# A gated mix of a long convolution and a dense ReLU block: three eras instead of two, the last one's first layer by Strassen products

## The chip, the cores and the metric

The kernel runs on one core of a Trainium2 chip. The metric is the device time of one execution in microseconds (us), the median of several runs. The engines are named as in the profile: PE is TensorE's matmuls, PEld its weight loads, DVE is VectorE, ACT ScalarE, POOL GpSimd, SP the engine that issues the DMAs.

## The reference

Tokens S = 2048, channels D = 512, hidden width 1792, all in float32. Cut to what matters:

```
k_shift = sum over t in 0..3 of k_pad[:, t:t+S, :] * shift_k[:, 3-t]     # causal taps
kv = k_shift * v
y  = causal convolution over S of kv with ssm_k, per channel (by FFT of length 2S)
a  = q * (y + kv * ssm_D)
b  = relu(q @ w1) @ w2                       # x of both branches is q
g  = sigmoid((q * gate_w).sum(-1))
out = g * a + (1 - g) * b
```

## The kernel before, in words

**Dense branch.** The 2048 tokens are four chunks of 512, the hidden width 14 blocks of 128. A float32 matrix is split into a high and a low part with short mantissas (`split`, L295: the high part by a cast on ScalarE, L299; the low part by a subtraction on VectorE or, as its `alt`, on POOL, L302), and each product is three matmuls: high by high, high by low, low by high. `mlp1` (L369) computes one hidden block for one chunk: 4 k parts by 3 matmuls of 128x128 by 128x512, 12 in all, L376 to L378. `mlp1_out` applies ReLU: ScalarE writes the high part `hh` (L389), VectorE the low part `hl` (L392). `mlp2` (L398) computes 128 tokens by 512 outputs of one chunk, adding up over the blocks of the era, 3 matmuls a block, L406 to L408. An era is a set of blocks: there are two of 7 (`ERAS`, L292), the second runs over the chunks in reverse (`CHUNKS`, L293), so the chunk at the turn needs no new load of x. Results of the first era are copied to `y` by ScalarE (L421); those of chunk 0 go out to DRAM (`yd`, L426) and come back before the end (`again`, L790). In the second era VectorE adds to `y` (L429), except for the last chunk, whose results are used from PSUM.

**Convolution branch.** It runs beside the dense one as a transform in steps. `conv_x` (L491) forms taps and product on VectorE; `stage1` (L451) transforms h and x of 8 groups by small tiled matmuls (L459) and stores to the DRAM buffer `sa`. `conv_mid` (L558) runs for 8 groups of frequencies: forward matmuls `f_h` and `f_x` (L575, 64 together), complex products on VectorE (L609, L617), their sums on POOL (L623), and, two groups later, the inverse `iv` (L652, 32 matmuls), whose results `bv` leave PSUM half by ScalarE (L662), half by VectorE (L664) to the DRAM buffer `sb`. A closing call takes the last two inverses in one go. `conv_end` (L687) loads from `sb`, runs the last small matmuls `cy` (L727) in two runs of 8 groups, and forms gate and output on VectorE (L709, L737, L740, L677).

**Order.** All operations are entered in a list with a cost, a rank, dependencies and buffers, and `Plan.order` (L97) runs a list schedule over them by its cost constants: at each instant the engine takes the ready operation of lowest rank. The program is then written in that order, so each engine's queue is static. Dense matmuls have ranks (1, count); conv matmuls rank (0, ...), so they go first once ready. A pair of stage-one operations waits, up to `LONG` by the planner's clock, for a partner and for the end of a `mlp2` run (`twin`, L113), because tiled matmuls are costly to switch to. Buffers are rings, named by tag, with the counts in `room`; a ring with `fifo` is filled in the order in which its users were entered. There are eight PSUM banks (`cv`). Conv tiles lie in a pool that `phase` (L435) swaps: phase 1 for stage one (input ring `in`, 7 tiles), phase 2, after the last store to `sa`, for the middle (`r` 4 and `yr` 2 tiles), phase 3, after the last store to `sb`, for the end (`br`, 4 tiles of 8 KB per partition).

## Time and profile before

| what | value |
|---|---|
| median of 3 runs | 385.86 us (385.71 to 385.87) |
| span of the profiled execution, first to last instruction | 384.2 us |
| mean granted clock of TensorE in it | 0.999 |
| DMA in it | 92.51 MB, mean 241 GB/s |
| busy: ACT | 128.8 us |
| busy: POOL | 91.5 us |

The profiled execution's own time is known only as its span; the median of the timed runs is 1.66 us above that. In the profile "L376" is line 376 of the kernel, "x160" a count, and an arrow names what is written and what is read. In the rows by line, busy time and mean duration of one instruction (ns) are followed by the idle time ahead of them and by what ended it. In the rows by stage each engine has its busy time and, in brackets, its instructions; the last three numbers are the granted clock, the busy share of the DMA engines and GB/s. Rows of the timeline give start, duration, engine, line and operation.

### The profile page before, as it was taken

Reading aid. Unit: us, or ns where it says so; the run is one execution under the profiler, and the core shown is the slowest. Engines: PE = TensorE matmul, PEld = TensorE weight load, DVE = VectorE, ACT = ScalarE, POOL = GpSimd, SP = SyncE. Lnnn points to the kernel's source line nnn. Section 1 sums busy time; section 2 is a strip of 40 time slices with the busy share of each in tenths; the row PEclk is TensorE's granted clock in tenths of the full one; section 3 lists DMA queues with packets and bytes.
Section 4 is the critical chain, followed back from the end, with each engine's and each line's share of the span. In section 5 each row is a group of like instructions: output and inputs, shape, how many; then the busy total and the mean of one; then the engine's idle time right before and its main releaser. Section 6 shows DMA issues by size and latency. Waiting matters only on the chain.

```text
span 384.2 us, 6567 instructions
## 1 busy us (share of the span) xinstructions
PE 379.8 (99%) x2505; PEld 273.8 (71%) x2505; DVE 266.7 (69%) x356; ACT 128.8 (34%) x242; POOL 91.5 (24%) x77
## 2 busy tenths in 40 slices
PE   9999999999999999999999999999999999999996
PEld 5888788668877788788655765565587788688684
DVE  4698999797989028114799687897872347687691
ACT  5643524573147525533224022313400333012100
POOL 0000000000000000000199968866995001000000
PEclk9999999999999999999999999999999999999999
DMA  7997893898648763589867876686460798399331
GB/s 274 368 317 255 298 351 113 293 333 323 208 121 330 295 234 109 185 296 275 285 203 238 307 265 227 241 308 232 139 204 3 241 342 320 120 325 357 117 124 56
DMA packets 43474, 92.51 MB, mean 241 GB/s; under 512 B 4625, under 2 KB 7201, under 8 KB 43442
## 3 DMA queue, kind: packets, MB, share of 16 engines
q1 hardware_dynamic: 43090, 91.77, 68.8%
q8 instruction: 20, 0.33, 0.4%
q10 hardware_dynamic: 288, 0.26, 0.2%
q14 instruction: 12, 0.10, 0.1%
q0 software_dynamic: 64, 0.05, 0.0%
HBM read 61.66 MB, written 30.41 MB: 240 GB/s over the span
## 4 chain that ended last, share of the span: by engine, by line
PE 99%; DVE 0%; DVEq 0%; issue 0%
PE m L406 14%; PE m L407 13%; PE m L408 13%; PE m L376 13%; PE m L377 12%; PE m L378 12%; PE iv L652 4%; PE f_h L575 4%; PE f_x L575 4%; PE m L362 3%; PE s1x L459 2%; PE s1h L459 2%; PE cy L727 2%; PE warm L753 1%; DVE o L677 0%; DVEq L887 0%
## 5 line engine op out<-in xcount | busy, mean ns | idle before, releaser
L623 POOL TENSOR_TENSOR p<-p,ha 128x512 f32<-128x512 f32 x32 | 41.1, 1308 | 202.2 <-DVE ha L617 201.6
L406 PE MATMUL m<-w1h_h,hh 128*128 128x512 f32 x224 | 88.7, 396 | 0.0
L407 PE MATMUL m<-w1l_l,hh 128*128 128x512 f32 x224 | 87.3, 390 | 0.0
L408 PE MATMUL m<-w1h_h,hl 128*128 128x512 f32 x224 | 87.2, 389 | 0.0
L389 ACT ACTIVATE hh<-m 128x512 fp32r<-128x512 f32 x56 | 33.1, 598 | 126.4 <-PE m L378 122.1
L392 DVE SCALAR_TENSOR_TENSOR hl<-m,hh 128x512 fp32r<-128x512 f32 x56 | 38.3, 688 | 44.5 <-ACT hh L389 44.3
L376 PE MATMUL m<-xh_h,w0h_h 128*128 128x512 f32 x160 | 63.0, 394 | 0.0
L377 PE MATMUL m<-xl_l,w0h_h 128*128 128x512 f32 x160 | 62.3, 390 | 0.0
L378 PE MATMUL m<-xh_h,w0l_l 128*128 128x512 f32 x160 | 62.3, 389 | 0.0
L406 PEld LDWEIGHTS m<-w1h_h,hh 128*128 128x128 f32 x224 | 42.0, 188 | 19.1 <-ACT ev L464 6.5
L408 PEld LDWEIGHTS m<-w1h_h,hl 128*128 128x128 f32 x224 | 42.0, 188 | 9.0
L407 PEld LDWEIGHTS m<-w1l_l,hh 128*128 128x128 f32 x224 | 42.1, 188 | 8.3
L376 PEld LDWEIGHTS m<-xh_h,w0h_h 128*128 128x128 f32 x160 | 30.0, 188 | 11.1 <-issue 4.2
L378 PEld LDWEIGHTS m<-xh_h,w0l_l 128*128 128x128 f32 x160 | 30.0, 188 | 6.4
L377 PEld LDWEIGHTS m<-xl_l,w0h_h 128*128 128x128 f32 x160 | 30.0, 188 | 6.0
L518 DVE TENSOR_TENSOR acc<-acc,tmp 128x1024 f32<-128x1024 f32 x24 | 29.3, 1222 | 0.6
L302 DVE TENSOR_TENSOR w1l_l<-raw,w1h_h 128x512 fp32r<-128x512 f32 x14 | 9.4, 686 | 17.7 <-ACT w1h_h L299 17.7
L662 ACT COPY bv<-iv 128x512 f32<-128x512 f32 x16 | 8.7, 589 | 37.1 <-PE iv L652 31.9
L515 DVE TENSOR_TENSOR tmp<-in,sht_sht 128x512 f32<-128x512 f32 x32 | 20.8, 685 | 0.1
L623 POOL TENSOR_TENSOR p<-p,qa 128x512 f32<-128x512 f32 x16 | 20.7, 1317 | 0.0
L617 DVE TENSOR_TENSOR ha<-f_x,ha 128x1024 f32<-128x1024 f32 x16 | 19.5, 1221 | 1.3 <-DVE qb L617 0.5
L623 POOL TENSOR_TENSOR p<-p,qb 128x512 f32<-128x512 f32 x16 | 20.3, 1290 | 0.0
(72 smaller groups left out, 468.1 us busy)
## 6 DMA issues: line engine op xcount, KB each, us to landing
sa<-ev SPq DMA_DIRECT2D x64, 256.0 KB, 3.0
sb<-bv SPq DMA_DIRECT2D x32, 256.0 KB, 3.4
br<-sb SPq DMA_DIRECT2D x16, 512.0 KB, 6.8
raw<-xp SPq DMA_DIRECT2D x28, 256.0 KB, 4.2
raw<-w SPq DMA_DIRECT2D x24, 256.0 KB, 3.8
r_x<-sa SPq DMA_DIRECT2D x12, 512.0 KB, 5.1
in<-kn SPq DMA_DIRECT2D x10, 512.0 KB, 5.0
r_h<-sa SPq DMA_DIRECT2D x10, 512.0 KB, 6.3
```

The lines of the kernel that those rows point to most:

```text
L376: mm(ps, part("h", f, k), T["x", "h", xe, c, k], start=k == 0, stop=False)
L377: mm(ps, part("h", f, k), T["x", "l", xe, c, k], start=False, stop=False)
L378: mm(ps, part("l", f, k), T["x", "h", xe, c, k], start=False, stop=k == 3)
L389: nc.scalar.activation(tile_of(("hh", era, c, f), "hh", dt=F32R, p=mp, bufs=HB), T["m1", era, c, f], AF.Relu)
L392: nc.vector.scalar_tensor_tensor(tile_of(("hl", era, c, f), "hl", dt=F32R, p=mp, bufs=HB), T["m1", era, c, f], 0.0, T["hh", era, c, f].bit ...
L406: mm(ps, T["hh", era, c, f][:, z], T["w", "h", 1, f], start=f == fs[0], stop=False)
L407: mm(ps, T["hh", era, c, f][:, z], T["w", "l", 1, f], start=False, stop=False)
L408: mm(ps, T["hl", era, c, f][:, z], T["w", "h", 1, f], start=False, stop=f == fs[-1])
L515: nc.vector.tensor_tensor(o[:, z], T["k", c + (j == 0) + part][:, u], T["sht",][:, j * D:(j + 1) * D], op=OP.mult)
L518: nc.vector.tensor_tensor(T["acc", c], T["acc", c], T[dst], op=OP.add)
L575: mm(ps[b][32 * j:32 * j + 32, :], T[k("cf")][at, 64 * j + 32 * o:64 * j + 32 * o + 32], T[k("r", t, j // 2)][at, (j % 2) * D:(j % 2 + 1) ...
L623: nc.gpsimd.tensor_tensor(planes("p", dst, n), planes("p", dst, n), planes(src, u, n), op=OP.add if sign > 0 else OP.subtract)
```

## The change

There are three eras, of 5, 5 and 4 blocks; the second goes backwards over the chunks and the third forwards again. The second layer accumulates once per era. `y` stays in SBUF; the trip of chunk 0 through DRAM goes. In the third era the first layer isn't computed by `mlp1` but by `combine`, for each pair of chunks (c, d). There the weights of two blocks are seen as a 2 x 2 matrix A (blocks by halves of k) and x as a 2 x 2 matrix B (halves of k by chunks), and Winograd's form of Strassen's algorithm gives the four results from seven products of 6 matmuls each, for two u (pairs of blocks) in turn. Combinations t1 to t4 of x are formed on VectorE or POOL, s1 to s4 of the weights in `load_combined`, and each is split anew. The sums of products are kept by VectorE in SBUF (u2, u3) or finish a result (c21, c22, c12); p1 is copied by ScalarE. The x of the second pair lies in the phase-3 pool (ring `xs`), the first pair's in the ring `r`.

All conv loads use one ring `r` of 8 tiles of 4 KB outside the phase pools; a `br` load takes two of them. The loads of h and x in the middle wait for the stores of h or of x alone. The two closing inverses are separate calls, all `bv` leave PSUM by ScalarE, two of the sums of the last group run on VectorE, `conv_end` has four runs of 4 groups. Results of chunks 2 and 3 are used from PSUM in the last era. Buffers: `w0` 7 (WA), `w2` 5, `hh` 5, `t` 2, `q` 5. In the planner a waiting stage-one operation wakes when its time in `LONG` is over; the third entry of `LONG` goes from 12 to 0.

```diff
+            if op["pair"]:
+                event(now + LONG[op["pair"] - 1] + 0.01, "wake", op)
...
-    ERAS = [range(0, NF // 2), range(NF // 2, NF)]
-    CHUNKS = [list(range(NCHUNK)), list(range(NCHUNK))[::-1]]
+    ERAS = [range(0, 5), range(5, 10), range(10, NF)]
+    CHUNKS = [[0, 1, 2, 3], [3, 2, 1, 0], [0, 1, 2, 3]]
+    TURN = [None, 3, 0]
...
+    def combine(p, c, d, cgate):
+        pairs = [tuple(ERAS[2][2 * u:2 * u + 2]) for u in range(2)]
...
+        for nm, src, k0 in (("b22", d, 2), ("b12", d, 0), ("b11", c, 0), ("b21", c, 2)):
...
+            raws[nm] = add("SP", ISSUE, (-47, rank[1])[p], go, [cgate if p else xgate[0]], [tag], dma=2 * ROW, fifo=[tag])
...
+            made[dst] = add("DVE", dve_time(2 * D), rank, go, deps, port=True, alt=("POOL", 2.39))
...
+        minus("t3", "b22", "b12", [raws["b22"], raws["b12"]], "b22")
+        minus("t1", "b12", "b11", [made["t3"], raws["b11"]], "b12")
+        minus("t2", "t3", "b11", [made["t1"], *own("b11")], "b11", 1)
+        minus("t4", "b21", "t2", [made["t2"], raws["b21"], *own("b21")], "b21")
...
+        for nm, ld in (("t2", "t4"), ("t3", "t2"), ("t4", "t4"), ("t1", "t2"), ("b22", None)):
+            if not ld:
+                made[ld] = add("SP", ISSUE, rank[-1], again, [cgate, made["t2"]], ["xs"], dma=2 * ROW, fifo=["xs"])
+            for i in range(2):
+                cut(nm, i, made[ld], [tag if ld else "xs"] if i else [])
...
+                    ps = bank(key) if first and not i else T[key]
+                    mm(ps, w_at("h", wn, u, i), x_at("h", xn, i), start=first and not i, stop=False, skip_group_check=True)
+                    mm(ps, w_at("h", wn, u, i), x_at("l", xn, i), start=False, stop=False, skip_group_check=True)
+                    mm(ps, w_at("l", wn, u, i), x_at("h", xn, i), start=False, stop=last and i == 1, skip_group_check=True)
+
+                prev = add("PE", 3 * MM, (1, at[0] - back, u, i), go, [wpart[wn, u], xl[xn, i], prev, *([] if i else deps)],
+                           ["cv"] if first and not i else (), ["x"] if u else (), ends=bool(i))
...
+        x = [product(n("X", u), u, "a11", "b11", [], True, False, 0 if p else BACK) for u in us]
+        p1 = [add("ACT", act_time(D, True), (0, -1000 + at[0]), lambda u=u: nc.scalar.copy(tile_of(n("p1", u), "raw", p=mp), T[n("X", u)]), [x[u]], ["raw"], fifo=["raw"]) for u in us]
...
+        x = [product(n("X", u), u, "a12", "b21", [p1[u]], False, True, 0 if p else BACK) for u in us]
...
+        z = [product(n("Z", u), u, "s2", "t2", [], True, False) for u in us]
+        u2 = [summed(n("u2", u), "raw", n("Z", u), n("p1", u), [z[u], p1[u]]) for u in us]
...
+        z = [product(n("Z", u), u, "s3", "t3", [u2[u]], False, False) for u in us]
+        u3 = [summed(n("u3", u), "sv", n("Z", u), n("p1", u), [z[u], cgate]) for u in us]
...
+        z = [product(n("Z", u), u, "a22", "t4", [u3[u]], False, True) for u in us]
+        c21 = [summed(n("p1", u), None, n("Z", u), n("p1", u), [z[u]], ["cv"]) for u in us]
...
+        for s in range(4):
+            mlp2(2, c, s, [pairs[u][e] for e in range(2) for u in us])
...
+        y = [product(n("Y", u), u, "s1", "t1", [], True, False, 1.5) for u in us]
+        c22 = [summed(n("u3", u), None, n("Y", u), n("u3", u), [y[u]]) for u in us]
...
+        y = [product(n("Y", u), u, "s4", "b22", [c22[u]], False, True) for u in us]
+        c12 = [summed(n("u2", u), None, n("Y", u), n("u2", u), [y[u]], ["cv"]) for u in us]
...
+        for s in range(4):
+            mlp2(2, d, s, [pairs[u][e] for e in (1, 0) for u in us])
...
+    def load_combined(rank):
...
+            s1 = combo("s1", 0, (1, 0), (1, 1), 1, [lg], ["raw"])
+            s3 = combo("s3", 0, (0, 0), (1, 0), -1, [lf, lg, own], ["raw"])
+            s2 = combo("s2", 1, (0,), (0, 0), -1, [s1, lf])
+            s4 = combo("s4", 1, (0, 1), (1,), -1, [s2, s3], (), ["raw"])
...
-            nc.sync.dma_start(rows(tile_of(key, "in", R * D)), src)
+            nc.sync.dma_start(rows(tile_of(key, "r", R * D, p=mp)), src)
...
-            return add("SP", ISSUE, rank + 0.1 * u + (0 if t == "h" else 1), ld, [gate], [tag], dma=2 * ROW, fifo=[tag])
+            return add("SP", ISSUE, rank + 0.1 * u + (0 if t == "h" else 1), ld, stores[t], ["r"], dma=2 * ROW, fifo=["r"])
...
-            if j % 2:
+            if True:
...
-    for g in range(NJ // 4 + 1):
+    for g in range(NJ // 4 + BEHIND):
...
-    for m in range(2):
-        conv_end(order_n[8 * m:8 * m + 8], p3)
+    for m in range(4):
+        conv_end(order_n[4 * m:4 * m + 4], p3)
...
+DIRECT = 2, 3
+BACK = 2.5
+XR = 540.0, 704.5
+WA = 7
-LONG = 50.0, 50.0, 12.0, 0.0
+LONG = 50.0, 50.0, 0.0, 0.0
```

## The prediction

> **What bounds the kernel now.** I read the head of the page first, then the busy time by stage, then TensorE's own timeline, and only after that the groups of the other engines. The page:

> ```profile
> span 384.2 us, 6567 instructions
> PE 379.8 (99%) x2505; PEld 273.8 (71%) x2505; DVE 266.7 (69%) x356; ACT 128.8 (34%) x242; POOL 91.5 (24%) x77
> PE   9999999999999999999999999999999999999996
> PE 99%; DVE 0%; DVEq 0%; issue 0%
> ```

> The chain that ended last is TensorE and nothing else. By stage (0 to 100 us: first stage of the long convolution beside the dense layers; 100 to 183; 183 to 299: its middle; then its end), columns are length, PE, PEld, DVE, ACT and POOL busy:

> ```profile
> 0.00:100.00 100.00, 99.22 (x520) 75.61 (x521) 83.47 (x103) 46.54 (x84) 0.88 (x5) 1.00 0.84 295
> 100.00:183.00 83.00, 83.00 (x457) 64.20 (x456) 41.21 (x54) 38.94 (x72) 0.00 (x0) 1.00 0.66 223
> 183.00:299.00 116.00, 116.00 (x1080) 71.25 (x1078) 90.14 (x93) 28.34 (x51) 89.30 (x71) 1.00 0.64 218
> 299.00:384.20 85.20, 81.57 (x460) 62.78 (x452) 51.92 (x107) 15.02 (x36) 1.29 (x1) 1.00 0.63 226
> ```

> TensorE is full in every stage; VectorE (DVE) is at 83% in the first and 78% in the third. A busy PE could still hide waits shorter than a matmul's modelled end (0.39 us against a spacing of 0.23), so I read starts, not durations:

> ```profile
> 183.08 0.39 PE L378 MATMUL m<-xh_h,w0l_l 128*128 128x512 f32 x1
> 183.40 1.95 PE L575 MATMUL f_h<-r_h,cf 64*32 64x512 f32 x32
> 185.14 1.92 PE L575 MATMUL f_x<-r_x,cf 64*32 64x512 f32 x32
> 187.00 0.50 PE L376 MATMUL m<-xh_h,w0h_h 128*128 128x512 f32 x1
> 187.34 0.40 PE L377 MATMUL m<-xl_l,w0h_h 128*128 128x512 f32 x1
> ...
> 190.34 0.39 PE L378 MATMUL m<-xh_h,w0l_l 128*128 128x512 f32 x1
> ...
> 193.06 0.39 PE L378 MATMUL m<-xh_h,w0l_l 128*128 128x512 f32 x1
> ...
> 380.18 0.39 PE L408 MATMUL m<-w1h_h,hl 128*128 128x512 f32 x1
> 380.61 0.88 DVE L677 SCALAR_TENSOR_TENSOR o<-m,gs,t 128x256 f32<-128x256 f32 x2 [4.01 <-PE m L408]
> ```

> From 190.34 to 193.06 are twelve matmuls: 2.72/12 = 0.2267 us each, the price of a dense matmul. One visit to the convolution's tiled matmuls costs, beyond the matmuls: 183.08 to 183.40 is 0.09 over a step; the second group of 32 takes 1.86 to the next start where the first took 1.74, so 0.12; 187.00 to 187.34 is 0.11 over a step. Together **0.32 us per visit**. After the last matmul starts, 4.0 us remain, which the change leaves. So time is the number of dense matmuls, plus the tiled ones, plus visits, plus whatever waits appear; now there are practically none. The span is 384.2, the median of the timed runs 385.86: 1.66 us lie around the span, and I keep them.

> **The change part by part.**

> *Strassen products (removed: matmuls).* Four blocks over four chunks take 4 x 4 x 12 = 192 matmuls in the first layer. The new form has 7 products of 6 matmuls (two k parts, three high/low terms), for two u and two chunk pairs: 7 x 6 x 2 x 2 = 168. The second layer keeps its count, merely cut into three accumulations per output instead of two. So 24 x 0.2267 = **-5.44 us**, all of it on the bound.

> *More visits (added).* By the kernel's loops there are now 8 in stage one, 8 in the middle, one closing inverse that does two groups, 2 at the end. The closing inverse becomes two visits and the end four (four runs of four instead of two of eight): +3 x 0.32 = **+0.96 us**. Stage one goes in twos (h and x, 32 matmuls a visit); the planner's new "wake" can let one go alone once it has waited 50 us by its clock. Bounds: 0 to 8 more visits, 0 to 2.56 us; I take 0, because rests between second-layer runs become more frequent (a chunk of 5 blocks is 5 x 24 x 0.2267 = 27 us, one of 7 is 38), so pairing gets easier.

> *VectorE and its helpers.* The rows for the sizes that occur:

> ```profile
> L392 DVE SCALAR_TENSOR_TENSOR hl<-m,hh 128x512 fp32r<-128x512 f32 x56 | 38.3, 688 | 44.5 <-ACT hh L389 44.3
> L512 DVE TENSOR_TENSOR tmp<-in,sht_sht 128x1024 f32<-128x1024 f32 x8 | 9.8, 1221 | 0.1
> L299 ACT CAST xh_h<-raw 128x512 fp32r<-128x512 f32 x27 | 15.1, 619 | 2.3 <-DMA raw<-xp 2.2
> L664 DVE COPY bv<-iv 128x512 f32<-128x512 f32 x16 | 10.4, 685 | 10.9 <-PE iv L652 7.9 <-DMA sb<-bv 2.9
> L662 ACT COPY bv<-iv 128x512 f32<-128x512 f32 x16 | 8.7, 589 | 37.1 <-PE iv L652 31.9 <-issue 3.4 <-DMA sb<-bv 1.6
> L429 DVE TENSOR_TENSOR y<-m,y 128x512 f32<-128x512 f32 x12 | 8.2, 686 | 11.7 <-PE m L408 11.7
> L623 POOL TENSOR_TENSOR p<-p,qa 128x512 f32<-128x512 f32 x16 | 20.7, 1317 | 0.0
> ```

> On VectorE: 16 evictions bv go to ScalarE, -10.4. A third accumulation adds 16 sums of 0.69: +11. Split low parts: 24 more of x (52 against 28): +16.5. Sums of products, 5 x 2 x 2 = 20 of 0.69: +13.7. Combinations of x, 8 at 1.22: +9.8. Of weights, 8 of 128x256 plus more splits, by half and full widths of the same slope: about +5.5. Two of the last group's sums leave POOL: +1.4 on VectorE, -2.6 on POOL. Total about +47: 267 becomes 314 of some 380 us, 83%, if none is given away; splits and combinations (32 us) may go to POOL, which idles outside the middle. ScalarE takes 16 x 0.589, 24 x 0.619 and some copies: 129 to about 157, 41%. Neither becomes the bound as a sum, so both are costed at nothing on the end; what hides them is TensorE's work. Where that cover is missing is the next part.

> *Hand-offs between products (added waits).* Products share a bank: the copy p1 or the sum u2, u3, c22 must read it before the next product accumulates. TensorE's queue is in order, so everything behind that matmul waits too. The other u covers: from the last start of one product to the first of its successor lie seven steps, 1.59 us. The chain is 0.43 (380.18 to 380.61) plus 0.69 plus an estimated 0.1 back to TensorE, 1.22; slack 0.37 us if VectorE is free. Around p1 and c22 the ranks (BACK 2.5, and 1.5) put a second-layer run of 12 matmuls, 2.7 us, between; only Z to Z to Z is uncovered: 2 gaps x 2 pairs x 2 u = 8 hand-offs. VectorE meets them while doing one of 0.69 to 1.22, and it doesn't break off. With the busy share of 0.8 the mean rest of such an op is 0.8 x 0.69 / 2 to 0.8 x 1.22 / 2, so 0.3 to 0.5 us, about the slack, so a hand-off is late by perhaps 0.1: **+0.8 us** taken for all eight. Bounds: 0 (all on time, or other matmuls put there), and 8 x (1.22 - 0.37) = 6.8 (a whole 1024 op ahead of each).

> *Two engines on SBUF.* VectorE's splits and combinations read two SBUF operands, as POOL's sums do. What that costs when they meet:

> ```profile
> 203.30 3.78 POOL L302 TENSOR_TENSOR xl_l<-raw,xh_h 128x512 fp32r<-128x512 f32 x3
> 207.04 2.99 POOL L623 TENSOR_TENSOR p<-p,qa 128x512 f32<-128x512 f32 x2
> ...
> 206.28 1.36 DVE L302 TENSOR_TENSOR xl_l<-raw,xh_h 128x512 fp32r<-128x512 f32 x1
> ```

> VectorE's split took 1.36 instead of 0.69, and POOL's two sums 2.99 instead of 2 x 1.317 at most. [...] If all 40 new ops of that sort (24 splits, 8 + 8 combinations) met POOL, VectorE would gain 40 x 0.67 = 27 us: 341, still under TensorE. The planner keeps such pairs apart in its order, and most of the new ones come after POOL's sums have ended. I take 0.

> *Loads.* The y round trip goes (8 transfers of 256 KB, 2.1 MB), ten of 512 KB for x come (5.2 MB): +3.1 MB, 3%, with SP issuing two more. The y sums of chunk 0 no longer wait for a reload. Conv loads in one ring, outside the phase pools, may start before the phase turns; no wait of TensorE's is on them now, so that gains nothing by itself. At the start the second layer begins one block after the first four instead of three:

> ```profile
> 6.79 4.93 SPq L288 DMA_DIRECT2D raw<-w  x4
> ...
> 15.53 1.00 SPq L288 DMA_DIRECT2D raw<-w  x2
> 15.90 0.23 PE m L376
> ...
> 21.63 0.69 DVE L302 TENSOR_TENSOR w1l_l<-raw,w1h_h 128x512 fp32r<-128x512 f32 x1
> ```

> The fifth block starts at 15.90 and takes 12 x 0.2267 = 2.7, so the second layer would start near 18.6. The four weights issued from 6.79 were two of each layer; now all can be second layer, and the fifth takes the place of the one ready at 21.63 + 0.69 = 22.3, needed at 18.6 + 4 x 0.68 = 21.3. Upper bound 1.0 us; below, 0, as the four outputs can all begin with blocks 0 to 3 (10.9 us of work). I take 0.

> *The sum.* 384.2 - 5.44 + 0.96 + 0.8 = 380.5 span; with 1.66 around it **382.2 us**.

> **The rivals.**

> *Part of the gain is eaten* (16%): singles in stage one (+2.56 at most) or hand-offs late by 0.4 each (+3.2). For: VectorE at 83% before 100 us, where both its queue and TensorE's order are static. Time 383.3 to 385.1.

> *Nothing is left* (7%): waits of 4.5 us in all cancel 5.44 - 0.96 = 4.48. Time 385.1 to 386.6. This also covers the case that the change doesn't do what it says on the bound: 24 matmuls go, but TensorE stands still in their place.

> *Slower: hand-offs decide* (9%). VectorE's conv work (up to 1.22, in the middle 2.3 for a 2048 op) lies ahead of each of the eight sums; 8 x 0.85 = 6.8 against 4.48: 388.2. The point from which it decides is 4.48/8 = 0.56 us late per hand-off. Against: before, VectorE at 83% in the first stage never held TensorE up.

> *Slower: the second pair waits for the end of the convolution* (4%). Its x tiles lie in the pool that opens only when the last bv is stored:

> ```profile
> 298.21 6.23 SPq L659 DMA_DIRECT2D sb<-bv  x8
> 304.53 0.38 SPq L689 DMA_DIRECT2D gwt_gwt<-gw  x1
> 306.60 0.88 SPq L702 DMA_DIRECT2D br<-sb  x2
> ...
> in<-hn SPq DMA_DIRECT2D x8, 512.0 KB, 4.7
> ```

> By these rows, loads come at 306.6, land 4.7 later and are split in 0.62 + 0.69: 313. The pair needs 84 x 0.2267 = 19 us plus 96 x 0.2267 = 22 us for its second layer, so it must begin near 380 - 41 = 339: 26 us of slack. It decides if the convolution ends 26 us later than now, then one for one; a delay of 31 us gives 386.9. Stage one and the middle run on VectorE, POOL and the same DMA, and bv leaves VectorE, so I expect it no later. A gap that long has a second price:

> ```profile
> 0.78 3.95 PE warm L753 x9
> ```

> The first nine took 0.44 us each, twice 0.2267. [...]

> **How the numbers follow.** The forecast with waits of 0 to 1.9 us has 64%: 381.4 to 383.3; 382.2 is its likeliest value. A measurement here can tell about 0.2%, 0.77 us: below 385.09 is faster, above 386.63 slower. Faster 64 + 16 = 80%; same 7%; slower 9 + 4 = 13%. The range: low 380.8 (no new waits, and two visits fewer than counted), high 386.4, leaving the slower rivals outside.

> **What would show it.** PE x2481 instead of x2505, dense starts still 0.227 apart, 22 visits, four cy groups of 32. Strassen hand-offs: gaps ahead of the Z products, each with a VectorE sum as its releaser; in sum under 2 us. VectorE near 300 us, POOL's gaps outside the middle filled by splits. The first matmul of the second pair must come tens of us after the last sb store. Wrong, if PE's idle time between its first and last matmul is above 4 us, if a slice of the page's PE row before the last falls under 9, or if more than 25 visits occur.

## The result, and the profile after

The changed kernel takes 393.14 us (median), the kernel before 385.87 in the runs beside it: a ratio of 1.0185, 95% interval 1.017 to 1.0199. It is slower by 7.3 us where I had forecast 3.7 faster, and lies outside my range. The span of the profiled execution is 391.4 us against 384.2.

From the page after: its head, the busy shares of three engines and the granted clock in 40 slices, and the chain that ended last:

```profile
span 391.4 us, 6670 instructions
PE 382.4 (98%) x2481; PEld 270.4 (69%) x2481; DVE 311.6 (80%) x405; ACT 153.5 (39%) x290; POOL 117.9 (30%) x92
PE   9999999999999999999999999999999889999995
DVE  4698999699599741249888897899957989999972
POOL 0000000000000000004898999997113815143100
PEclk9999999999999999999999999999999989999999
PE 89%; DVE 8%; issue 2%; ACT 0%; DVEq 0%
```

The 24 matmuls are gone (2481 instead of 2505). But the chain is no longer TensorE alone: 8% of it is VectorE. TensorE's holes are in the 32nd and 33rd slice (303 to 323 us), the dip of the clock is in the second of them, and POOL, idle in the last stage before, now works there. A slice under 9 before the last was one of the signs of being wrong that I had named. The last two stages, columns as before:

```profile
183.00:299.00 116.00, 115.89 (x1021) 72.26 (x1019) 98.16 (x105) 43.98 (x82) 87.25 (x70) 1.00 0.73 252
299.00:391.40 92.40, 84.30 (x441) 60.76 (x439) 79.05 (x135) 23.74 (x51) 28.23 (x16) 0.97 0.52 181
```

The last stage holds 79.05 us of VectorE where there were 51.92, and 28.23 of POOL where there was 1.29. TensorE's largest wait is there. In the timeline its end is marked by the idle time ahead, counted from the modelled end of the matmul before, and by the releaser:

```profile
311.49 0.39 PE L591 MATMUL m<-w1l_l,hh 128*128 128x512 f32 x1
314.27 0.50 PE L592 MATMUL m<-w1h_h,hl 128*128 128x512 f32 x1 [2.39 <-DVE hl L474]
...
315.14 0.63 PE L592 MATMUL m<-w1h_h,hl 128*128 128x512 f32 x1
315.57 0.63 PE L590 MATMUL m<-w1h_h,hh 128*128 128x512 f32 x1
...
328.75 0.40 PE L591 MATMUL m<-w1l_l,hh 128*128 128x512 f32 x1
330.03 0.50 PE L592 MATMUL m<-w1h_h,hl 128*128 128x512 f32 x1 [0.88 <-DVE hl L474]
```

From start to start 2.78 us pass instead of 0.23, and then, from 315.14, the matmuls are 0.43 apart: half rate. Seven such starts, and the slower one on either side of them, cost 1.6 us. VectorE and POOL around that wait, from the same timeline:

```profile
307.99 0.67 DVE L465 TENSOR_TENSOR raw<-Z,raw 128x512 f32<-128x512 f32 x1
308.51 5.15 POOL L403 TENSOR_TENSOR xs_b<-xs_b,xs_b 128x1024 f32<-128x1024 f32 x2
308.71 2.75 DVE L880 CUSTOM_DVE_ANT_0 j<-q,gwt_gwt 128x512 f32<-128x512 f32 x1
...
311.39 2.82 DVE L474 SCALAR_TENSOR_TENSOR hl<-raw,hh 128x512 fp32r<-128x512 f32 x1
```

POOL forms two combinations t of the second pair, 2.40 and 2.68 us. The gate sum j, with q and the gate's weights both in SBUF, takes 2.75 us instead of 0.69 and ends 0.55 us after the first of them. The low part hl behind it takes 2.82 and ends 0.55 us after the second. Its two operands are in SBUF too, because a finished Strassen result lies there, while the low parts of the plain layer read PSUM. The sum raw<-Z,raw, one operand in PSUM, ran at 0.67 beside an earlier POOL op. That is the wait of TensorE, 2.55 us beyond the usual 0.23 from start to start. Others, counted in the same way: 0.47 at 306.76, 1.05 at 328.75, 0.52 and 0.36 at 351. In sum these five are 4.95 us. Four of them end with a low part hl ahead of a second-layer matmul, the last with a VectorE sum (raw<-Z,raw) ahead of a Strassen product.

### The profile page after: what moved, and what is told of

The parts are those of the page before. It is cut to its first block, busy times and chain, and to the rows that moved or that the text cites. A ratio compares the mean times of both kernels' runs of the same rounds, so it can differ in the third digit from the quotient of the medians.

```text
span 391.4 us, 6670 instructions
## 1 busy us (share of the span) xinstructions
PE 382.4 (98%) x2481; PEld 270.4 (69%) x2481; DVE 311.6 (80%) x405; ACT 153.5 (39%) x290; POOL 117.9 (30%) x92
## 4 chain that ended last, share of the span: by engine, by line
PE 89%; DVE 8%; issue 2%; ACT 0%; DVEq 0%
PE m L590 12%; PE m L592 12%; PE m L591 12%; PE m L382 9%; PE m L383 8%; PE m L384 8%; PE f_h L747 4%; PE iv L826 4%; PE f_x L747 4%; PE m L368 3%; DVE j L880 3%; PE s1x L634 2%; PE s1h L634 2%; DVE t L908 1%; DVE hl L474 1%
## 5 line engine op out<-in xcount | busy, mean ns | idle before, releaser
L576 DVE SCALAR_TENSOR_TENSOR hl<-m,hh 128x512 fp32r<-128x512 f32 x40 | 27.2, 686 | 25.3 <-ACT hh L573 25.3
L382 PE MATMUL m<-xh_h,w0h_h 128*128 128x512 f32 x96 | 38.0, 396 | 0.0
L383 PE MATMUL m<-xl_l,w0h_h 128*128 128x512 f32 x96 | 37.4, 390 | 0.0
L384 PE MATMUL m<-xh_h,w0l_l 128*128 128x512 f32 x96 | 37.4, 390 | 0.0
L604 DVE TENSOR_TENSOR y<-m,y 128x512 f32<-128x512 f32 x24 | 16.4, 685 | 14.9 <-PE m L592 14.8
L382 PEld LDWEIGHTS m<-xh_h,w0h_h 128*128 128x128 f32 x96 | 18.0, 188 | 7.8 <-issue 1.7
L690 DVE TENSOR_TENSOR tmp<-r,sht_sht 128x512 f32<-128x512 f32 x32 | 20.9, 685 | 0.2
L384 PEld LDWEIGHTS m<-xh_h,w0l_l 128*128 128x128 f32 x96 | 18.0, 188 | 3.8
L383 PEld LDWEIGHTS m<-xl_l,w0h_h 128*128 128x128 f32 x96 | 18.0, 188 | 3.6
L787 DVE TENSOR_TENSOR ha<-f_x,ha 128x1024 f32<-128x1024 f32 x16 | 19.5, 1221 | 0.8
L639 ACT COPY ev<-s1x 128x512 f32<-128x512 f32 x32 | 16.4, 601 | 9.1 <-PE s1x L634 9.1
## 6 DMA issues: line engine op xcount, KB each, us to landing
r_h<-sa SPq DMA_DIRECT2D x16, 512.0 KB, 5.4
r_x<-sa SPq DMA_DIRECT2D x16, 512.0 KB, 6.9
r<-sb SPq DMA_DIRECT2D x16, 512.0 KB, 6.2
r<-kn SPq DMA_DIRECT2D x10, 512.0 KB, 4.8
```

The costliest lines, as they stand in the source:

```text
L382: mm(ps, part("h", f, k), T["x", "h", xe, c, k], start=k == 0, stop=False)
L383: mm(ps, part("h", f, k), T["x", "l", xe, c, k], start=False, stop=False)
L384: mm(ps, part("l", f, k), T["x", "h", xe, c, k], start=False, stop=k == 3)
L576: nc.vector.scalar_tensor_tensor(tile_of(("hl", era, c, f), "hl", dt=F32R, p=mp, bufs=HB), T["m1", era, c, f], 0.0, T["hh", era, c, f].bit ...
L690: nc.vector.tensor_tensor(o[:, z], T["k", c + (j == 0) + part][:, u], T["sht",][:, j * D:(j + 1) * D], op=OP.mult)
```

## The experiments

The theory (A): POOL, which takes splits and combinations of the Strassen part, reads SBUF and so holds up VectorE's ops with two SBUF operands on the way to TensorE. The rivals: VectorE simply has too much to do in the last stage (B); the eras, rings and loads cost it (C); POOL's results come late by themselves (D). Each experiment is the changed kernel with the edit shown.

**e1: the third era's first layer plain.**

```diff
-            if era == 2:
-                continue
...
-                if era:
-                    load_combined(535)
-                for i in range(era, 2):
+                for i in range(2):
...
-    for p in range(2):
-        combine(p, *CHUNKS[2][2 * p:2 * p + 2], p3)
```

> The third era's first layer is computed plainly again (192 matmuls, x loaded and split as in the other eras); three eras, the one ring and the four closing runs stay. Theory A (POOL's added SBUF work holds up VectorE at the Strassen hand-offs) and rival B (VectorE has too much work in the last stage, POOL or not) both put the whole loss into the Strassen part: 386.8 us, the kernel before plus three visits of 0.32. Rival C (the eras, the smaller rings or the shared load ring cost it): 390 or more.

Measured 388.86 us, ratio to the kernel before 1.0072 (1.0057 to 1.0087). So 4.3 of the 7.3 us lie in the Strassen part, and 2.9 don't: neither 386.8 nor 390. With 22 visits instead of 19, three times 0.32 would explain 0.96. (In the traces one visit cut in two costs 0.27 more: the closing inverse takes 3.94 us from dense start to dense start before, its two halves 2.22 each in the changed kernel, less one step of 0.23. So 0.8 for three.) A further 1.1 us is a wait in the third visit of the middle, the first that contains an inverse; e6 takes it up.

**e2: POOL writes and doesn't read.**

```diff
+            if eng == "POOL":
+                nc.gpsimd.memset(tile_of(lo, tag + "l", dt=F32R, bufs=bufs, p=p).bitcast(F32), 0.0)
+                return
...
+                if eng == "POOL":
+                    nc.gpsimd.memset(o, 0.0)
+                    return
...
```

> Same order of all instructions, but wherever POOL formed a low part or a combination of x, it now only fills the tile with zeros and reads nothing (these parts of the result are left out). VectorE keeps all its work. A: the slow low parts hl<-raw,hh fall from 1.22 to 0.69 us and the gate sums from 1.09 to 0.69, TensorE's waits after 300 us fall from about 9 to 2 or less: 385 to 387. B: 391 or more, as VectorE's work is the same.

Measured 384.0 us, 0.9945 of the kernel before (0.9929 to 0.9962): 9.1 us less than the changed kernel, with the same order of instructions and all of VectorE's work. The groups of the changed kernel that read two SBUF operands:

```profile
L880 DVE CUSTOM_DVE_ANT_0 j<-q,gwt_gwt 128x512 f32<-128x512 f32 x16 | 17.4, 1087 | 0.2
L474 DVE SCALAR_TENSOR_TENSOR hl<-raw,hh 128x512 fp32r<-128x512 f32 x8 | 9.6, 1223 | 0.0
L465 DVE TENSOR_TENSOR raw<-Z,raw 128x512 f32<-128x512 f32 x8 | 5.5, 684 | 0.8 <-PE Z L455 0.7
```

and the same two in e2:

```profile
L886 DVE CUSTOM_DVE_ANT_0 j<-q,gwt_gwt 128x512 f32<-128x512 f32 x16 | 11.0, 686 | 0.2
L480 DVE SCALAR_TENSOR_TENSOR hl<-raw,hh 128x512 fp32r<-128x512 f32 x8 | 5.3, 684 | 0.0
```

Gate sums and low parts are back at 0.69 us. The sum with one PSUM operand (third row of the changed kernel) never was slow. In e2 no wait of 0.2 us or more is left between dense matmuls, and none starts at half rate. As a cause of the loss B falls: the same operations on VectorE hide wholly.

**e3: short gate sums.**

```diff
-                nc.vector.tensor_tensor_reduce(tile_of(k("j"), "j"), T[k("q")], T["gwt",], ...
+                nc.vector.tensor_tensor_reduce(tile_of(k("j"), "j")[:, :8], T[k("q")][:, :8], T["gwt",][:, :8], ...
```

> Same order; each gate sum goes over 8 columns instead of 512 (the rest of the gate's sum is left out), so VectorE loses 16 ops of 0.69 us, those that meet POOL first. A: the collisions that remain are those of the low parts themselves with POOL's 128x1024 ops; waits after 300 us about 4: 388. B: 10 us less VectorE work ahead of the hand-offs takes nearly all waits: 385 to 386.

Measured 388.56 us, 1.0047 (1.0022 to 1.0073). Four of the six runs lie at 388.5 to 388.7, with a mean granted clock of 0.994; two lie at 386.0 and 386.8, with 0.998 and 0.999. In the profiled execution, one of the four, a single wait remains, 1.85 us beyond the usual 0.23 at 324.68, behind an output that met POOL, and eight starts at half rate after it, 1.6 us. Whether the half rate follows would account for most of the difference between the two sorts of runs, though no trace of the shorter sort was kept. So the median alone doesn't tell A (388) from B (385 to 386). The trace does: the short gate sums still take 0.35 us each, 5.7 in all against 11.0 in e2, and VectorE is busy for 299.2 us here and for 300.3 in e2. With about the same VectorE time, a wait behind a collision is left here and none in e2. That speaks for A again.

**e4: the planner keeps them apart.**

```diff
-            prev = add("DVE", ..., [] if i else ["o"], give if last else ())
+            prev = add("DVE", ..., [] if i else ["o"], give if last else (), port=key[0] == "y")
...
-            g = add("DVE", dve_time(D) + 0.06, rank, gate_sum, [q, gload[0]])
+            g = add("DVE", dve_time(D) + 0.06, rank, gate_sum, [q, gload[0]], port=True)
```

> Gate sums and the outputs that read two SBUF tiles are marked for the planner, so that it sets none of them beside a POOL op; it then leaves more combinations and splits to VectorE. A: collisions go, waits that are left come from VectorE's own load: 388 to 390. B: VectorE gets more work at the hand-offs: 393 or more.

Measured 388.85 us, 1.0075 (1.0059 to 1.0091), in the middle of what A expected. Gate sums are at 0.69 us again; of the low parts some still meet POOL (mean 0.88). The waits that are left are 2.1 us at a cy visit near 343 and 1.6 after it. From 337 to 351 the chain is almost all VectorE's, one op of ordinary length after the other; a part of it:

```profile
339.54 0.68 DVE xl_l_t L308
340.23 0.60 DVE j L880
340.83 0.01 DVE gs L880
340.83 0.60 DVE xl_l_t L308
341.44 0.60 DVE hl L474
342.04 0.60 DVE xl_l_t L308
342.64 0.49 DVE hl L474
```

Here B's mechanism holds, though not its 393: with splits and combinations that POOL had, VectorE is late by its load.

**e5: fills as long as the subtractions.** As e2, each fill three times.

> As e2_pool_writes_only, but each fill is done three times, so that POOL is busy as long per step as with its subtractions (0.53 x 3 = 1.6 us against 1.3, 0.95 x 3 = 2.9 against 2.67) and hands its results over no earlier (the same parts of the result are left out). Theory A (what costs is POOL reading SBUF while VectorE reads two SBUF operands): as e2, 384 to 385. Rival D (POOL's results simply come late, and e2 was fast because its fills are short): 390 or more.

Measured 384.34 us, 0.9954 (0.994 to 0.9967). POOL was busy as long, and no wait of 0.2 us was left between dense matmuls. One thing differs: a fill need not wait for the cast ahead of it, so the splits near 305 were done 0.8 to 1.0 us earlier than in the changed kernel. D falls all the same, since in the changed kernel's trace only a wait of 0.2 us (347.47) ended with a result of POOL's.

**e6: bv on both engines, plain era.** The edit of e1, and

```diff
-            if True:
+            if j % 2:
```

> The plain third era of e1 with the evictions bv again half on VectorE. Theory E: of the 2.9 us that e1 lies above the kernel before, 0.96 are three more visits and 1.3 the wait in the third visit of the middle, where four bv in a row on ScalarE free the banks late: 387.5. Rival F: that wait comes from VectorE (y sums of the second era ahead of the products that free the banks): 388.9 or more, as VectorE gets more.

Measured 387.5 us, 1.0038 (1.0026 to 1.005), 1.4 less than e1. F falls. TensorE in the third visit of the middle, in e1:

```profile
193.51 1.97 PE L826 MATMUL iv<-p,cc 32*64 32x512 f32 x32
195.41 2.67 PE L747 MATMUL f_h<-r_h,cf 64*32 64x512 f32 x25
197.59 0.59 PE L747 MATMUL f_x<-r_x,cf 64*32 64x512 f32 x1
...
195.54 1.07 ACT L836 COPY bv<-iv 128x512 f32<-128x512 f32 x2 [7.32 <-PE iv L826]
197.12 1.08 ACT L836 COPY bv<-iv 128x512 f32<-128x512 f32 x2
```

and in e6:

```profile
193.01 1.97 PE L826 MATMUL iv<-p,cc 32*64 32x512 f32 x32
194.91 1.95 PE L747 MATMUL f_h<-r_h,cf 64*32 64x512 f32 x32
196.66 1.06 PE L747 MATMUL f_x<-r_x,cf 64*32 64x512 f32 x16
...
195.08 1.07 ACT L836 COPY bv<-iv 128x512 f32<-128x512 f32 x2 [7.36 <-PE iv L826]
```

From f_h to f_x were 2.18 us, now 1.75, and in e1 f_h's last matmuls came even later, among f_x. The banks of the next products come free when the four bv have left. On ScalarE alone the last two start 1.58 us after the first two, with a copy of f_h between them; in e6 VectorE takes two in the meantime, from 195.44 to 196.71. From the last dense start ahead of such a visit to the first behind it pass 6.96 us in e1 and 5.81 in e6, as in the kernel before. C is right by these 1.4 us and the visits. Of the 0.5 us that e6 lies above the kernel before beyond 0.96, half is the end: after the last matmul starts 4.26 us remain in e6, 4.01 before. The rest stays unexplained.

**e7 and e11: both effects alone.** A small kernel: VectorE ops of 128x512 beside four POOL sums or ten fills of 128x1024, and stretches of 40 matmuls with waits between.

> No part of the reference is computed. VectorE runs 128x512 ops of three sorts (two SBUF operands; one PSUM and one SBUF) alone and beside POOL's 128x1024 sums or fills. If the two engines exclude each other for a whole op: 0.69 alone, about 2.5 to 3 for one beside a POOL sum, PSUM form and fills without effect. If they share: 1.0 to 1.4. TensorE runs matmuls in stretches with waits of about 0.8, 1.4, 2.0, 2.6, 3.2 and 4.4 us between. If a wait of 1.85 us is enough for the half clock (as in e3): 8 or so slow matmuls at 0.43 us from the third wait on; if it takes 3.4: only after the last.

> No part of the reference is computed. As e7, with its order kept, so that VectorE's ops with one operand in PSUM and POOL's fills are measured too (in e7 they ran by themselves). If only POOL's reading against two SBUF operands counts: the PSUM form stays at 0.69 us beside POOL's sums, and two SBUF operands stay at 0.69 beside fills. The waits of TensorE are now 1.3, 1.95, 1.95, 2.6, 2.6 and 1.95 us: if what decides is the length alone, those of 1.95 are all without the half clock, as in e7; if it is where the wait falls, some have it.

In e7 six two-operand ops took 10.62 us beside four POOL sums instead of 4.33. e11, VectorE's timeline: ten ops with two SBUF operands beside sums, ten with one operand in PSUM beside sums, ten with two beside fills; then POOL's sums against the first and against the PSUM form:

```profile
18.59 13.52 DVE L49 TENSOR_TENSOR both<-y,z 128x512 f32<-128x512 f32 x10
46.00 7.21 DVE L53 TENSOR_TENSOR one<-ps,z 128x512 f32<-128x512 f32 x10
54.63 7.23 DVE L49 TENSOR_TENSOR both<-y,z 128x512 f32<-128x512 f32 x10
...
19.42 9.24 POOL L64 TENSOR_TENSOR pool<-x 128x1024 f32<-128x1024 f32 x4
46.51 7.81 POOL L64 TENSOR_TENSOR pool<-x 128x1024 f32<-128x1024 f32 x4
```

Six alone took 4.3, so 0.72 each. Only two SBUF operands beside a reading POOL are slow: 6.3 us lost over four sums, 1.6 a sum, and POOL loses too (2.31 instead of 1.95 a sum). In the changed kernel each VectorE op with two SBUF operands that started during a POOL op ended 0.55 us after it, and e11's times agree: from 0.55 us after the last sum (29.21) to the end of the ten (32.11) is room for just four of 0.72. The clock, from the chain of e11: stretches of 40 matmuls, each behind its wait.

```profile
37.69 9.37 PE ps L35 x40
49.03 10.98 PE ps L35 x40
62.62 11.01 PE ps L35 x40
76.24 11.00 PE ps L35 x40
89.20 9.37 PE ps L35 x40
```

The waits ahead of them, as idle time in the profile, were 1.97, 1.98, 2.63, 2.62 and 1.97 us. The two above 2.6 cost 1.6 us each; of the three near 2 one did, and two did not. In e7 waits of 0.68, 1.32 and 1.97 cost nothing, 2.62 and 3.27 cost 1.6 each, 4.57 cost 2.5. So it isn't the length alone: near 2 us it depends on where the wait falls.

The granted clock of the traces shows where. Every half-rate stretch between matmuls lasts 3.41 us (in e11 from 49.96 to 53.37, in the changed kernel from 314.96 to 318.38) or, after the wait of 4.57, twice that; and it starts a whole number of 3.41 us periods after the clock first rose to full (in the changed kernel 91 of them, from 4.34 to 314.96). In e11 the wait of 1.98 that cost lies within one such period, 46.55 to 49.96. The two that cost nothing are cut by the bounds of periods at 36.31 and 87.51. At full rate, and over all these traces, a period with at most 1.4 us without a matmul was never followed by half rate, one with 1.98 or more always; of two periods with 1.7 us, one was (e3) and one wasn't (e11). This is read off the traces; no run moved a wait to test it.

**e8, e9, e10: the same work, planned anew.** All three have e4's edit, and the changes below. PATIENCE is how long a VectorE op may wait before it holds POOL back, SAFE a slack behind an engine; XR and CUT are ranks of the combinations and of their splits, BACK is how far the first pair's first products are moved ahead.

```diff
 e8:  PATIENCE = 0.5 -> 5.0;  SAFE ... DVE=0.4 -> 0.2
 e9:  bv: if j % 2;  XR = 550.0, 702.5;  CUT = (0, -899), (1, 704.0);  SAFE ... PE1=0.1, DVE=0.2
 e10: bv: if j;  BACK = 4.5;  PATIENCE = 5.0;  CUT = (0, -899), (1, 701.0);  SAFE ... DVE=0.2
```

> Same work as the changed kernel; the planner keeps gate sums and two-operand outputs apart from POOL as in e4, takes 0.2 instead of 0.4 us of slack behind VectorE and lets a waiting VectorE op hold POOL back only after 5 us. A: almost no waits after 300 us, so the gain of the Strassen products shows: 383.5 to 385. B (VectorE's load decides whatever the order): 388 or more, as e4.

> All of the Strassen part, gate sums and two-operand outputs kept apart from POOL by the planner, bv half on VectorE again, and other ranks (XR, CUT) and slacks (SAFE). Theory: e8 still had 1.3 us of wait in the third visit of the middle, which the bv on both engines removes as in e6, and some 1.5 us after 300 us, which the order removes at best: 383.3 to 385. If VectorE's load decides whatever the order (B): 386 or more, as it gets 16 more ops of 0.69 us.

> As e9 with only every fourth bv on VectorE, and e8's PATIENCE; the first product of the first pair goes further back (BACK 4.5). Theory: most of the 1.3 us wait goes, as the bank freed first no longer waits in ScalarE's row: 384 to 385.5. B: 386 or more.

Measured: e8 386.08 us, 1.0002 (0.9993 to 1.001), no difference, a microsecond more than expected; e9 385.39, 0.9988 (0.9979 to 0.9997), also above its 385 (one low part still met POOL and took 2.85 us, and TensorE waited 1.5); e10 383.71, 0.9947 (0.9935 to 0.996), better than expected and faster than both kernels. Its page, and its last stage:

```profile
span 381.9 us, 6675 instructions
PE   9999999999999999999999999999999999999995
DVE  5699999699599942228798899699987798999986
POOL 0000000000000000000989999999422544020000
```

```profile
299.00:381.90 82.90, 77.86 (x433) 58.62 (x431) 74.66 (x139) 21.74 (x48) 14.50 (x10) 1.00 0.53 184
```

POOL still works in the last stage, 14.5 us instead of 28.2: of the four long combinations two are left on POOL, of thirteen splits nine. Two waits are left between dense matmuls, 0.9 us at a Strassen product behind its VectorE sum (299.6), which stood behind a gate sum of 1.78 us that met POOL, and 0.4 behind a low part; the clock stays full until the last matmul. e8 has the same two waits. The 2.4 us between e8 and e10 lie in the middle: the six visits with inverse and forward products take 37.55 us in e8, with all bv on ScalarE, and 35.19 in e10.

## Why the prediction was wrong

**The step that failed** is "Two engines on SBUF ... I take 0". I had the row that shows the effect (1.36 us instead of 0.69), and e11 shows it alone (ten such ops take 13.52 us beside four sums, 7.23 beside fills). But I priced it as busy time of VectorE, 27 us at most, "still under TensorE". It strikes single ops, and some of them stand on a hand-off: then each microsecond of it is one of TensorE's. Two reasons given there were wrong as well. "Most of the new ones come after POOL's sums have ended": but POOL itself took splits and combinations, as my paragraph on VectorE had said it might, and read SBUF far into the last stage. "The planner keeps such pairs apart": it does so only for marked operations, and gate sums and outputs were not marked; before, POOL had 1.29 us of work in the last stage. Nor had I seen that the low parts of the Strassen results read SBUF. These were marked (L478) and met POOL all the same: the gate sum ahead of the slowest took 2.75 us where the planner counts 0.71, and the low part slid onto the next POOL op. The price is the difference to e2: **9.1 us** against my 0.

Of these 9.1 us of TensorE's path, the five waits are 4.95, the half rate 1.6 and a wait within the last cy visit 0.9, together 7.5. Three waits of 0.2, and 0.1 more from the first start behind a wait to the next (0.34 instead of 0.23), make most of the rest.

**Hand-offs from Z to Z** were sized at 0.8 us with 6.8 as the worst. The 0.1 us from VectorE back to TensorE in their chain was my estimate; in the changed kernel it is 0.06 (hl ends at 314.21, the matmul starts at 314.27) and 0.05 (the sum ends at 352.37, Z starts at 352.42). In e2, where nothing collides, they cost nothing that can be seen. In the changed kernel one of the five waits was there (0.36 at 351.83), the others at the second layer, on low parts. My slower rival (9%) named VectorE's lateness and got the sign, with the wrong place and cause; its 388.2 was 5 us short.

**The half clock** was put on a long gap at the phase change alone. That a gap between matmuls brings it was my assumption then: in the trace of before the nine matmuls at 0.44 us are the first of the program. That rival did not occur, but half rate did, and cost 1.6 us after 2.39 us of idle time; the longest wait, 4.57 us in e7, cost 2.5. The 3.4 us that e7's expectation weighs against 1.85 were an assumption as well. The runs show half rate from 1.7 us (e3), so they decide against 3.4 as a threshold on a single gap; what has that length in the traces is the half-rate stretch itself, 3.41 us.

**The evictions bv** were "costed at nothing", with TensorE's work as the cover. That was wrong by 1.4 us (e6 against e1): the banks they leave late are needed later in the same visit. In e2's trace it is more: the six visits with inverse and forward products take 6.97, 5.81, 5.87 and three times 6.08 us, against 5.81 each before, 2.0 us in all.

**What held.** The 24 matmuls: e2 against e1 is -4.9 us beside my -5.44; of the half microsecond between, 0.48 are two visits of the middle that take 6.08 us in e2 and 5.81 and 5.87 in e1. The visits are 22; the three more cost 0.8 rather than 0.96. The loads and the start cost nothing seen. The second pair did not wait for the convolution. The whole without collisions, e2's 384.0, lies 1.8 us above my 382.2, and as the 0.8 for hand-offs isn't in it, 2.6 have to be found. The bv are 2.0 of them, and 0.4 is the end: after the last matmul starts 4.38 us remain, where I had kept 4.0. The small rest I cannot place.

## What to carry to other kernels

When work is given to POOL because it idles, look at what VectorE does at that time and where its operands are: here an op with two SBUF operands lasted until POOL's was over (2.75 us beside one of 2.40), one with an operand in PSUM did not (0.72 us in e11 beside sums of 1.95). Price such a collision where the op stands, on the way to the bound engine, not in the sum of busy time. When an order is planned by costs, every operation that can collide has to be known to the plan, and those that never did before a change are the ones that are missing.
